# First chunks of an mLSTM and MLP-mixer kernel: zero fills ahead of the exponentials, gate subtractions on GpSimd, k q products ahead of phi, q factors sooner

## The chip, the cores and the metric

The kernel runs on one core of a Trainium2 chip. The metric is the device time of one execution in microseconds; before the change the median of three runs is 426.94 us (426.52 to 427.03). Five engines work in their own order and wait for one another by semaphores: TensorE (PE; its weight loads are listed as PEld), VectorE (DVE), ScalarE (ACT), GpSimd (POOL) and SyncE (SP), which issues nearly all DMAs.

## The reference

An mLSTM with exponential gates, whose output is the input x of a token mixer and a channel mixer.

```python
B, H, S, D = 4, 8, 768, 40
for t in range(S):
    m_new = np.maximum(f_gate[:, :, t] + m, i_gate[:, :, t])
    f_stab = np.exp(f_gate[:, :, t] + m - m_new)
    i_stab = np.exp(i_gate[:, :, t] - m_new)
    C = f_stab * C + i_stab * outer(v_t, k_t)
    n = f_stab * n + i_stab * k_t
    y[:, :, t] = sigmoid(o_t) * (C @ q_t) / max(abs(n @ q_t), 1)
x = y                                  # 4 x 768 x 320
h = np.maximum(x.T @ w_tok1, 0) @ w_tok2       # 768 -> 256 -> 768
u = x + h.T
out = u + np.maximum(u @ w_ch1, 0) @ w_ch2     # 320 -> 1536 -> 320
```

## The kernel before

The sequence is cut into six chunks of 128 steps for each of four batches; a unit (b, c) is a chunk c of batch b, and u0, u1, u2 are the first three chunks of batch 0. The gates of all batches and heads lie on 36 partitions with 768 steps along the free dimension. `gates_of` works out from them, on VectorE: a scan for the running maximum m (L120), f + m(t-1) - m(t) (L125, L127), a scan that sums these within a chunk to phi (L129), and b = i - m - phi (L131, L133). It is called once for chunks 0 and 1 and once for chunks 2 to 5. phi and b are the two planes of a tile z. `split` (L172) cuts z's fp32 values into three bf16 parts on three groups of partitions, so that products with 0/1 matrices can spread them exactly.

Within a chunk the output is (masked decay times k q products) times v, plus the carried state times q:

- `spread_late` and `spread_phi` (L163, L177) put phi(t) + b(s) of four heads into a PSUM bank "ps_phi" by products, with the mask of later steps; `spread_split` does both for eight heads. `prep_exp` (L287) takes the exponential on ScalarE into a tile dd.
- `st_s` (L307) makes the k q products "ps_sc" from a tile raw, in which two groups of four heads lie on partitions 0 to 39 and 64 to 103. With 64 rows in a product the rows up to 63 and 127 are read too, so `zero_rows` (L210) fills them with zeros, twice on ScalarE (raw1, raw2) and once on GpSimd (raw0).
- `st_p` (L317) multiplies dd by ps_sc on VectorE, in two halves; `st_pv` (L424) multiplies by v into "po".
- `spread_q` (L194) spreads phi for the factors of q into "ps_q" and, by `cols_w0`, the factors of k; `prep_q3` takes their exponentials on ScalarE (L274, and L142 for k) and scales q on GpSimd (L280); `prep_kw` scales k on GpSimd (L303).
- `st_state` (L368) multiplies the carried state by q (L378), and k by v for the new state (L386), which VectorE then masks and adds (L391, L395).
- `x0_ops` divides and multiplies by the sigmoid of the output gate (L476 to L485). `sigmoid` runs on ScalarE with another table of functions than the exponential, so a table load stands on either side.

PSUM is allotted in pools of two banks each: ps_h (phi, and the later ps_q), ps_s (k q products and chunk 1's ps_q), ps_m (po, pu, fillers), ps_acc. A tile waits for the readers of the tile that had its bank before.

All of it is written out in one fixed order of instructions for each engine: the order of the Python calls. The lines at the end of the function (from L862) are the first chunks' order; a loop then goes through chunks 1 to 5, while weights are loaded and decoded (`dec_...`), and the mixers of one batch run beside the attention of the next. `warm(n)` (L851) issues n products of zeros, whose result nobody reads, to keep TensorE at work.

DMAs on the sync queue are issued in program order too; each waits until the DMA eight places before it has landed, and until its target is free.

Of the kernel before, what the change touches and what calls it, by code (L numbers as in the profile page):

```python
# [18 lines left out]
L = 128  # L19
# [6 lines left out]
HP = 9  # L26
# [9 lines left out]
def kernel(ctx: ExitStack, tc: tile.TileContext, gates, qk, q3, kv, og,  # L36
# [16 lines left out]
    def load_sig(b, i):  # L53
        t = ap.tile([128, NC // 2, DM], F32, tag="sig", name="sig", bufs=3)
        nc.sync.dma_start(out=t, in_=og[b].rearrange("(c p) e -> p c e", p=128)[:, 3 * i:3 * i + 3, :])
        sig[(b, i)] = t
# [56 lines left out]
    bcol = wp.tile([128, NC, B * HP], F32, name="bcol")  # L113
    wcol = wp.tile([128, NC, B * HP], F32, name="wcol")

    def gates_of(c0, c1):
        lo, hi = c0 * L, c1 * L
        sl, sd, sm = slice(lo, hi), slice(max(lo, 1), hi), slice(max(lo, 1) - 1, hi - 1)
        v = nc.vector
        v.tensor_tensor_scan(m_t[:, sl], f_t[:, sl], i_t[:, sl],  # L120
                             -1e30 if lo == 0 else m_t[:, lo - 1:lo], op0=ALU.add, op1=ALU.max)
        yield
        if lo == 0:
            v.memset(f_t[:, 0:1], 0.0)
        v.tensor_tensor(f_t[:, sd], f_t[:, sd], m_t[:, sm], ALU.add)  # L125
        yield
        v.tensor_tensor(f_t[:, sd], f_t[:, sd], m_t[:, sd], ALU.subtract)  # L127
        yield
        v.tensor_tensor_scan(phi[:, sl], rst2[:, 0:hi - lo], f_t[:, sl], 0.0, op0=ALU.mult, op1=ALU.add)  # L129
        yield  # L130
        v.tensor_tensor(b_t[:, sl], i_t[:, sl], m_t[:, sl], ALU.subtract)  # L131
        yield
        v.tensor_tensor(b_t[:, sl], b_t[:, sl], phi[:, sl], ALU.subtract)  # L133
        yield

    def cols_w0(t, c):
        a, e = c * L, (c + 1) * L
        nc.tensor.matmul(t, top(z[:, 1, a:e]), id3, start=True, stop=False)
        nc.tensor.matmul(t, top(z[:, 0, e - 1:e]).to_broadcast([128, 128]), id3, start=False, stop=True)

    def cols_w0_out(t, c):
        nc.scalar.activation(wcol[:, c, 0:HP].rearrange("p (g i) -> p i g", g=3),  # L142
                             t.rearrange("p (i g) -> p i g", i=3), AF.Exp)
# [28 lines left out]
    def split(c0, c1, eng=nc.vector):  # L172
        p, r, r2 = (z[x:x + HP, :, c0 * L:c1 * L] for x in (0, 64, 96))
        eng.tensor_tensor(r, p, top(p), ALU.subtract)
        eng.tensor_tensor(r2, r, top(r), ALU.subtract)

    def spread_phi(r, c, h0=0, h1=H):  # L177
        zc = top(z[:, :, c * L:(c + 1) * L])
        for h in range(h0, h1):
            nc.tensor.matmul(r[h // 4][:, h % 4, :], id3[:, h:h + 1].to_broadcast([128, 128]),  # L180
                             zc[:, 0], start=False, stop=False)
            if h % 4 == 3:
                nc.tensor.matmul(r[h // 4], zc[:, 1], id3[:, h - 3:h + 1].unsqueeze(2).to_broadcast([128, 4, L]),
                                 start=False, stop=True)
# [25 lines left out]
    def zero_rows(i):  # L210
        for p in (32, 96):
            t = raws[i][p:p + 32].rearrange("p a h t -> p a (h t)")
            if i:
                nc.scalar.activation(t, zero[p:p + 32].unsqueeze(1).to_broadcast([32, 2, 512]), AF.Copy)
            else:
                nc.gpsimd.memset(t, 0.0)

    def sigmoid(b, r=range(2), part=slice(0, 3)):
        for i in r:
            t = sig[(b, i)][:, part]  # L220
            nc.scalar.activation(t, t, AF.Sigmoid)
# [65 lines left out]
    def prep_exp(u, hf):  # L287
        b, c = u
        dd = T[u]["dd"]
        if b == 0:  # L290
            nc.scalar.activation(dd[:, 4 * hf:4 * hf + 4, :], T[u]["phi"][hf], AF.Exp)  # L291
            return
        for h in range(4 * hf, 4 * hf + 4):
            nc.scalar.activation(dd[:, h, :], dd[:, h, :], AF.Exp, bias=bcol[:, c, HP * b + h:HP * b + h + 1])  # L294
# [9 lines left out]
                                wcol[:, c, HP * b:HP * b + H].unsqueeze(2).to_broadcast([128, H, D]), ALU.mult)  # L304
        t["kw"] = kw

    def st_s(u, mult=True, mid=iter(()), rows=64, pool=(ps_s, "s")):  # L307
        t = T[u]
        t["s"] = [pool[0].tile([128, 4, L], F32, tag=pool[1], name="ps_sc") for _ in range(2)]
        for h in range(4):  # L310
            for hf in range(2):
                r = t["raw"][64 * hf:64 * hf + rows]
                nc.tensor.matmul(t["s"][hf][:, h, :], r[:, 1, h, :], r[:, 0, h, :], start=True, stop=True)  # L313
        if mult:
            st_p(u, mid)
# [531 lines left out]
    def step(g, n=1):  # L847
        for _ in range(n):
            next(g, None)

    def warm(n, pool=(ps_m, "m"), z=zero):  # L851
        t = pool[0].tile([128, 512], F32, tag=pool[1], name="warm")
        for i in range(n):
            nc.tensor.matmul(t[:, 0:z.shape[-1]], z[:, 0:128], z, start=i == 0, stop=i == n - 1)  # L854
# [14 lines left out]
    load_sig(0, 0)  # L869
    load_qk(u1, 0)  # L870
    load_qk(u1, 1)
    load_sig(0, 1)
    load_kv(u1)
    q3s = {u1: load_q3t(u1)}

    T[u0]["phi"] = r = [spread_late(ps_h, "h") for _ in range(2)]
    warm(4)
    step(gates_of(0, 2), 9)
    split(0, 1)
    spread_phi(r, 0)  # L880
    t = ps_m.tile([128, HP], F32, tag="m", name="gw")
    cols_w0(t, 0)
    st_s(u0, mult=False, rows=D)
    split(1, 2)
    prep_exp(u0, 0)
    prep_exp(u0, 1)
    cols_w0_out(t, 0)
    zero_rows(2)
    prep_kw(u0)
    zero_rows(0)  # L890
    load_qk(u2, 0)
    load_qk(u2, 1)
    q3s[u2] = load_q3t(u2)
    load_kv(u2)
    dec_load(2)
    load_phi(us[3])
    load_qk(us[3], 0)
    load_qk(us[3], 1)
    spread_split(u1)
    st_s(u1, mult=False, pool=(ps_acc, "acc"))  # L900
    gr = gates_of(2, NC)
    step(gr, 3)
    st_p(u0)
    prep_exp(u1, 0)
    prep_exp(u1, 1)
    sigmoid(0)
    step(gr, 9)
    split(2, 3)
    warm(1)
    st_pv(u0)  # L910
    x0 = x0_ops(u0)
    step(x0, 2)
    st_state(u0)
    step(x0, 1)
    spread_q(u1, (ps_s, "s"))
    load_pq(u1, q3s[u1])
# [258 lines left out]
```

## Time and profile before

| what | value |
|---|---|
| median of 3 runs | 426.94 us |
| profiled execution | 426.81 us |
| its span, first to last instruction | 424.9 us |
| around the span | 1.9 us |
| granted TensorE clock, mean over the span | 1.000 |
| PE busy | 419.7 us (99%) |
| VectorE, ScalarE, GpSimd busy | 280.5, 184.0, 142.7 us |
| HBM read, written | 47.73 MB, 4.04 MB |

The table is from the page and the run list. The busy time of PE holds the fillers, and a product's end is modelled, so the starts of consecutive products tell more than their lengths. In a timeline a row merges instructions of one line that follow without a hole; a bracket gives the idle time ahead of it and what ended it. A wait that falls inside the modelled end of the previous product has no bracket; it shows as a late start.

### The profile page before, as it was taken

To read this page: it belongs to the slowest core of one execution; us is meant where nothing else is said; L and a number is where in the kernel's file an instruction comes from. 1 tells how busy PE (TensorE), PEld (TensorE's weight loads), DVE (VectorE), ACT (ScalarE), POOL (GpSimd) and SP (SyncE) were. 2 spreads that over 40 slices of the span, in tenths; PEclk is the share of its full clock that TensorE was granted. 3 is DMA by queue.
4 is the path that set the end of the run, shared out by engine and by line. 5 is a ranking of instruction groups with operands and counts; after the bars stand their busy time and mean duration, and the time that the engine had idled before them with its cause. 6 is when DMAs were issued, how large, how long until landed. Compare 5 with 4: busy or idle time off the path is not lost.

```text
span 424.9 us, 8988 instructions
## 1 busy us (share of the span) xinstructions
PE 419.7 (99%) x3510; PEld 396.8 (93%) x3510; DVE 280.5 (66%) x620; ACT 184.0 (43%) x426; POOL 142.7 (34%) x186
## 2 busy tenths in 40 slices
PE   8999999999999999999999999999999999999996
PEld 4888989999999999999999999999999999988996
DVE  8988565515876788799696698789796647111412
ACT  5978569893455635234323346334144112111211
POOL 7488488751544501241341230331350110000000
PEclk9999999999999999999999999999999999999999
DMA  7997658941876713333346121533320000000000
GB/s 218 278 292 268 241 170 290 272 147 52 253 199 195 213 39 104 123 117 125 95 154 195 35 93 43 137 116 93 119 86 32 0 23 12 0 2 0 35 28 31
DMA packets 24574, 52.34 MB, mean 123 GB/s; under 512 B 2565, under 2 KB 13325, under 8 KB 24533
## 3 DMA queue, kind: packets, MB, share of 16 engines
q1 hardware_dynamic: 24293, 51.61, 39.4%
q8 instruction: 27, 0.44, 0.5%
q10 hardware_dynamic: 240, 0.18, 0.1%
q14 instruction: 14, 0.11, 0.1%
HBM read 47.73 MB, written 4.04 MB: 122 GB/s over the span
## 4 chain that ended last, share of the span: by engine, by line
PE 94%; ACT 2%; POOL 2%; issue 0%; DVE 0%; POOLq 0%
PE acc L694 30%; PE ps_h L788 22%; PE ps_h L807 11%; PE ps_b L694 5%; PE ps_sc L313 5%; PE ps_a L694 5%; PE po L439 4%; PE po L409 3%; PE pu L386 3%; PE po L415 2%; PE po L378 1%; PE warm L854 1%; ACT dd L291 1%; PE ps_t L762 1%; PE ps_t L760 1%; PE ps_t L761 1%
## 5 line engine op out<-in xcount | busy, mean ns | idle before, releaser
L788 PE MATMUL ps_h<-uT,c1h 128*128 128x256 f32 x480 | 93.4, 282 | 0.0
L694 PE MATMUL acc<-c2h,gh 128*128 128x320 f32 x288 | 89.2, 319 | 0.0
L793 ACT ACTIVATE gh<-ps_h 128x512 fp32r<-128x512 f32 x48 | 28.7, 597 | 135.4 <-PE ps_h L788 132.4
L694 PE MATMUL acc<-c2l,gh 128*128 128x320 f32 x288 | 86.4, 309 | 0.0
L788 PEld LDWEIGHTS ps_h<-uT,c1h 128*128 128x128 f32 x480 | 76.9, 188 | 0.5
L788 PE MATMUL ps_h<-uT,c1l 128*128 128x256 f32 x288 | 74.3, 280 | 0.0
L794 DVE SCALAR_TENSOR_TENSOR gl<-ps_h,gh 128x512 fp32r<-128x512 f32 x48 | 33.0, 688 | 45.4 <-ACT gh L793 45.3
L694 PE MATMUL acc<-c2h,gl 128*128 128x320 f32 x288 | 61.8, 308 | 0.0
L694 PEld LDWEIGHTS acc<-c2h,gh 128*128 128x128 f32 x288 | 54.1, 188 | 1.6
L694 PEld LDWEIGHTS acc<-c2l,gh 128*128 128x128 f32 x288 | 54.2, 188 | 0.9
L788 PEld LDWEIGHTS ps_h<-uT,c1l 128*128 128x128 f32 x288 | 54.3, 188 | 0.0
L811 DVE SCALAR_TENSOR_TENSOR gl<-ps_h,gh 128x512 fp32r<-128x512 f32 x24 | 16.6, 692 | 49.0 <-ACT gh L810 49.0
L458 POOL TENSOR_TENSOR sig<-sig,ht 128x320 f32<-128x320 f32 x18 | 14.7, 816 | 98.4 <-DVE ht L419 90.0
L294 ACT ACTIVATE dd<-dd,bcol 128x128 f32<-128x128 f32 x144 | 45.8, 392 | 4.5 <-POOL dd L284 4.3
L694 PEld LDWEIGHTS acc<-c2h,gl 128*128 128x128 f32 x288 | 47.2, 188 | 0.0
L807 PE MATMUL ps_h<-uT,c1h 128*128 128x512 f32 x120 | 36.0, 394 | 0.0
L323 DVE TENSOR_TENSOR dd<-ps_sc,dd 128x512 f32<-128x512 f32 x48 | 30.9, 681 | 3.3 <-PE ps_sc L313 3.3
L509 POOL TENSOR_TENSOR xl<-x,xh 128x320 fp32r<-128x320 f32 x18 | 15.8, 877 | 51.1 <-DVE xh L507 46.3
L810 ACT ACTIVATE gh<-ps_h 128x512 fp32r<-128x512 f32 x24 | 14.3, 594 | 41.2 <-PE ps_h L807 41.2
L313 PE MATMUL ps_sc<-raw 64*128 64x128 f32 (+1 forms) x384 | 26.8, 282 | 0.0
L313 PEld LDWEIGHTS ps_sc<-raw 64*128 64x128 f32 (+1 forms) x384 | 23.1, 187 | 3.3 <-issue 1.7
L807 PEld LDWEIGHTS ps_h<-uT,c1h 128*128 128x128 f32 x120 | 22.1, 188 | 3.9
(152 smaller groups left out, 858.3 us busy)
## 6 DMA issues: line engine op xcount, KB each, us to landing
dd<-phi_d SPq DMA_DIRECT2D x18, 512.0 KB
wst<-in_wc_dram SPq DMA_DIRECT2D x22, 384.0 KB
kvt<-in_kv_dram SPq DMA_DIRECT2D x24, 324.0 KB
raw<-in_qk_dram SPq DMA_DIRECT2D x48, 160.0 KB
sig<-in_og_dram SPq DMA_DIRECT2D x8, 480.0 KB
out_dram<-x SPq DMA_DIRECT2D x24, 160.0 KB
q3t<-in_q_dram SPq DMA_DIRECT2D x20, 180.0 KB
wst<-in_wt_dram SPq DMA_DIRECT2D x8, 384.0 KB
```

Source lines behind the costliest of these rows:

```text
L294: nc.scalar.activation(dd[:, h, :], dd[:, h, :], AF.Exp, bias=bcol[:, c, HP * b + h:HP * b + h + 1])
L313: nc.tensor.matmul(t["s"][hf][:, h, :], r[:, 1, h, :], r[:, 0, h, :], start=True, stop=True)
L323: nc.vector.tensor_tensor(dd, t["s"][hf], dd, ALU.mult)
L439: nc.tensor.matmul(o, t["dd"][:, ROW[h], :], x, start=c == 0 and h == 0, stop=h == H - 1)
L458: nc.gpsimd.tensor_tensor(sg, sg, ht[:, :, 0:D], ALU.mult)
L509: nc.gpsimd.tensor_tensor(xl, x, f32(xh), ALU.subtract)
L694: nc.tensor.matmul(ps, a, m, start=(first and i == 0), stop=(last and i == n - 1))
L788: nc.tensor.matmul(ps[:, j, :], c1[x][:, a:a + 128], u[:, y, :], start=part is first and i == 0 and (order == 0 or j == 0), stop=i == len( ...
L793: nc.scalar.activation(gh, ps, AF.Relu)
L794: nc.vector.scalar_tensor_tensor(gl, ps, 0.0, f32(gh), op0=ALU.max, op1=ALU.subtract)
L807: nc.tensor.matmul(ps, c1[x][:, a:a + 128], u[:, :, y, :], start=n == 0, stop=n == len(todo) - 1)
L811: nc.vector.scalar_tensor_tensor(gl, ps, 0.0, f32(gh), op0=ALU.max, op1=ALU.subtract)
```

## The change

Nothing of what is computed changes. In the first chunks' order:

- both ScalarE zero fills stand at the start, ahead of chunk 0's exponentials; GpSimd's fill of raw0 is gone, and the products take 64 rows only in chunks 1, 2, 4 and 5 of batch 0, else the 40 filled by loads.
- the loads of q (for u1) go ahead of the second sigmoid load; the loads for u2 and the next chunk are issued earlier in the program.
- chunk 0's k q products stand ahead of the gates and of its phi products; one filler stands ahead of them where there were four.
- the gates of chunks 0 and 1 are split by one pair of operations on 256 steps instead of two pairs on 128.
- for the later chunks the scan of m still covers chunks 2 to 5; the f subtractions, phi scan and b subtractions are cut into chunk 2 (VectorE) and chunks 3 to 5, where GpSimd does the subtractions and VectorE the scan.
- chunk 1's `spread_q`, `prep_q3` and `prep_kw` stand ahead of chunk 0's `st_pv` and `st_state`, and the sigmoids behind chunk 1's q exponential; `x0_ops` of chunk 0 begins behind `st_state`.
- 13 fillers are left of 18.

On VectorE, from the scan of m for chunks 2 to 5 on, the kernel before has (z is the tile of phi and b, dd the decay, ps_sc the k q products):

```order
L120 SCALAR_TENSOR_TENSOR m_t<-f_t,m_t,i_t 36x512
L125 TENSOR_TENSOR f_t<-f_t,m_t 36x512
L127 TENSOR_TENSOR f_t<-f_t,m_t 36x512
L323 TENSOR_TENSOR dd<-ps_sc,dd 128x512 x2
L129 SCALAR_TENSOR_TENSOR z<-rst,f_t 36x512
L131 TENSOR_TENSOR z<-i_t,m_t 36x512
L133 TENSOR_TENSOR z<-z 36x512
L174 TENSOR_TENSOR z<-z 9x2x128
L175 TENSOR_TENSOR z<-z 9x2x128
```

and the changed kernel:

```order
L121 SCALAR_TENSOR_TENSOR m_t<-f_t,m_t,i_t 36x512
L128 TENSOR_TENSOR f_t<-f_t,m_t 36x128
L129 TENSOR_TENSOR f_t<-f_t,m_t 36x128
L132 SCALAR_TENSOR_TENSOR z<-rst,f_t 36x128
L137 TENSOR_TENSOR z<-i_t,m_t 36x128
L138 TENSOR_TENSOR z<-z 36x128
L324 TENSOR_TENSOR dd<-ps_sc,dd 128x512 x2
L132 SCALAR_TENSOR_TENSOR z<-rst,f_t 36x384
L178 TENSOR_TENSOR z<-z 9x2x128
L179 TENSOR_TENSOR z<-z 9x2x128
```

Chunk 0's multiplication (L323, now L324) had two operations between it and the scan and now has five shorter ones. On GpSimd, behind the constants, the kernel before has:

```order
L303 TENSOR_TENSOR kw<-kvt,wcol 128x320
L216 MEMSET raw_138 32x1024 x2
L279 COPY decay<-pq 120x3
L280 TENSOR_TENSOR q3t<-q3t,pq 120x384
L303 TENSOR_TENSOR kw<-kvt,wcol 128x320
L174 TENSOR_TENSOR z<-z 9x2x384
L175 TENSOR_TENSOR z<-z 9x2x384
```

and the changed kernel:

```order
L128 TENSOR_TENSOR f_t<-f_t,m_t 36x384
L129 TENSOR_TENSOR f_t<-f_t,m_t 36x384
L304 TENSOR_TENSOR kw<-kvt,wcol 128x320
L137 TENSOR_TENSOR z<-i_t,m_t 36x384
L138 TENSOR_TENSOR z<-z 36x384
L280 COPY decay<-pq 120x3
L281 TENSOR_TENSOR q3t<-q3t,pq 120x384
L304 TENSOR_TENSOR kw<-kvt,wcol 128x320
L178 TENSOR_TENSOR z<-z 9x2x384
L179 TENSOR_TENSOR z<-z 9x2x384
```

Two subtractions now stand ahead of chunk 0's scaled k (kw) and two behind it. On ScalarE, behind its first fill, the kernel before has:

```order
L291 ACTIVATE dd<-ps_phi 128x512 x2
L142 ACTIVATE wcol<-gw 128x3x3
L214 ACTIVATE raw_140<-zero 32x1024 x2
L291 ACTIVATE dd<-ps_phi 128x512 x2
L221 ACT_TABLE_LOAD
L221 ACTIVATE sig<-sig 128x960 x2
L274 ACT_TABLE_LOAD
L274 ACTIVATE pq<-ps_q 120x384
L142 ACTIVATE wcol<-ps_q 128x3x3
L291 ACTIVATE dd<-ps_phi 128x512 x2
```

and the changed kernel:

```order
L217 ACTIVATE raw_140<-zero 32x1024 x2
L292 ACTIVATE dd<-ps_phi 128x512 x2
L146 ACTIVATE wcol<-gw 128x3x3
L292 ACTIVATE dd<-ps_phi 128x512 x2
L275 ACTIVATE pq<-ps_q 120x384
L146 ACTIVATE wcol<-ps_q 128x3x3
L222 ACT_TABLE_LOAD
L222 ACTIVATE sig<-sig 128x960 x2
L292 ACT_TABLE_LOAD
L292 ACTIVATE dd<-ps_phi 128x512 x2
```

The q exponential of chunk 1 (pq) stood behind the sigmoids and stands ahead of them now, between the exponentials of chunks 1 and 2.

```diff
--- before.py
+++ after.py
@@ -113,25 +113,29 @@
     bcol = wp.tile([128, NC, B * HP], F32, name="bcol")
     wcol = wp.tile([128, NC, B * HP], F32, name="wcol")
 
-    def gates_of(c0, c1):
-        lo, hi = c0 * L, c1 * L
-        sl, sd, sm = slice(lo, hi), slice(max(lo, 1), hi), slice(max(lo, 1) - 1, hi - 1)
-        v = nc.vector
-        v.tensor_tensor_scan(m_t[:, sl], f_t[:, sl], i_t[:, sl],
-                             -1e30 if lo == 0 else m_t[:, lo - 1:lo], op0=ALU.add, op1=ALU.max)
-        yield
-        if lo == 0:
-            v.memset(f_t[:, 0:1], 0.0)
-        v.tensor_tensor(f_t[:, sd], f_t[:, sd], m_t[:, sm], ALU.add)
-        yield
-        v.tensor_tensor(f_t[:, sd], f_t[:, sd], m_t[:, sd], ALU.subtract)
-        yield
-        v.tensor_tensor_scan(phi[:, sl], rst2[:, 0:hi - lo], f_t[:, sl], 0.0, op0=ALU.mult, op1=ALU.add)
-        yield
-        v.tensor_tensor(b_t[:, sl], i_t[:, sl], m_t[:, sl], ALU.subtract)
-        yield
-        v.tensor_tensor(b_t[:, sl], b_t[:, sl], phi[:, sl], ALU.subtract)
-        yield
+    def cut(c0, c1):
+        return slice(c0 * L, c1 * L)
+
+    def gate_m(c0, c1):
+        lo = c0 * L
+        nc.vector.tensor_tensor_scan(m_t[:, cut(c0, c1)], f_t[:, cut(c0, c1)], i_t[:, cut(c0, c1)],
+                                     m_t[:, lo - 1:lo] if c0 else -1e30, op0=ALU.add, op1=ALU.max)
+
+    def gate_f(c0, c1, eng=nc.vector):
+        lo, hi = max(c0 * L, 1), c1 * L
+        if c0 == 0:
+            eng.memset(f_t[:, 0:1], 0.0)
+        eng.tensor_tensor(f_t[:, lo:hi], f_t[:, lo:hi], m_t[:, lo - 1:hi - 1], ALU.add)
+        eng.tensor_tensor(f_t[:, lo:hi], f_t[:, lo:hi], m_t[:, lo:hi], ALU.subtract)
+
+    def gate_phi(c0, c1):
+        nc.vector.tensor_tensor_scan(phi[:, cut(c0, c1)], rst2[:, 0:(c1 - c0) * L], f_t[:, cut(c0, c1)], 0.0,
+                                     op0=ALU.mult, op1=ALU.add)
+
+    def gate_b(c0, c1, eng=nc.vector):
+        sl = cut(c0, c1)
+        eng.tensor_tensor(b_t[:, sl], i_t[:, sl], m_t[:, sl], ALU.subtract)
+        eng.tensor_tensor(b_t[:, sl], b_t[:, sl], phi[:, sl], ALU.subtract)
 
     def cols_w0(t, c):
         a, e = c * L, (c + 1) * L
@@ -210,10 +214,7 @@
     def zero_rows(i):
         for p in (32, 96):
             t = raws[i][p:p + 32].rearrange("p a h t -> p a (h t)")
-            if i:
-                nc.scalar.activation(t, zero[p:p + 32].unsqueeze(1).to_broadcast([32, 2, 512]), AF.Copy)
-            else:
-                nc.gpsimd.memset(t, 0.0)
+            nc.scalar.activation(t, zero[p:p + 32].unsqueeze(1).to_broadcast([32, 2, 512]), AF.Copy)
 
     def sigmoid(b, r=range(2), part=slice(0, 3)):
         for i in r:
@@ -304,12 +305,12 @@
                                 wcol[:, c, HP * b:HP * b + H].unsqueeze(2).to_broadcast([128, H, D]), ALU.mult)
         t["kw"] = kw
 
-    def st_s(u, mult=True, mid=iter(()), rows=64, pool=(ps_s, "s")):
+    def st_s(u, mult=True, mid=iter(()), pool=(ps_s, "s")):
         t = T[u]
         t["s"] = [pool[0].tile([128, 4, L], F32, tag=pool[1], name="ps_sc") for _ in range(2)]
         for h in range(4):
             for hf in range(2):
-                r = t["raw"][64 * hf:64 * hf + rows]
+                r = t["raw"][64 * hf:64 * hf + (64 if u[0] == 0 and u[1] % 3 else D)]
                 nc.tensor.matmul(t["s"][hf][:, h, :], r[:, 1, h, :], r[:, 0, h, :], start=True, stop=True)
         if mult:
             st_p(u, mid)
@@ -861,6 +862,7 @@
 
     warm(10)
     zero_rows(1)
+    zero_rows(2)
     load_qk(u0, 0)
     load_qk(u0, 1)
     load_kv(u0)
@@ -869,56 +871,58 @@
     load_sig(0, 0)
     load_qk(u1, 0)
     load_qk(u1, 1)
+    q3s = {u1: load_q3t(u1)}
     load_sig(0, 1)
     load_kv(u1)
-    q3s = {u1: load_q3t(u1)}
-
-    T[u0]["phi"] = r = [spread_late(ps_h, "h") for _ in range(2)]
-    warm(4)
-    step(gates_of(0, 2), 9)
-    split(0, 1)
-    spread_phi(r, 0)
-    t = ps_m.tile([128, HP], F32, tag="m", name="gw")
-    cols_w0(t, 0)
-    st_s(u0, mult=False, rows=D)
-    split(1, 2)
-    prep_exp(u0, 0)
-    prep_exp(u0, 1)
-    cols_w0_out(t, 0)
-    zero_rows(2)
-    prep_kw(u0)
-    zero_rows(0)
     load_qk(u2, 0)
     load_qk(u2, 1)
     q3s[u2] = load_q3t(u2)
     load_kv(u2)
     dec_load(2)
     load_phi(us[3])
+
+    T[u0]["phi"] = r = [spread_late(ps_h, "h") for _ in range(2)]
+    warm(1)
+    st_s(u0, mult=False)
     load_qk(us[3], 0)
     load_qk(us[3], 1)
+    gate_m(0, 2)
+    gate_f(0, 2)
+    gate_phi(0, 2)
+    gate_b(0, 2)
+    split(0, 2)
+    spread_phi(r, 0)
+    t = ps_m.tile([128, HP], F32, tag="m", name="gw")
+    cols_w0(t, 0)
+    prep_exp(u0, 0)
+    prep_exp(u0, 1)
+    cols_w0_out(t, 0)
+    gate_m(2, NC)
+    gate_f(3, NC, nc.gpsimd)
+    gate_f(2, 3)
+    gate_phi(2, 3)
+    gate_b(2, 3)
+    prep_kw(u0)
     spread_split(u1)
     st_s(u1, mult=False, pool=(ps_acc, "acc"))
-    gr = gates_of(2, NC)
-    step(gr, 3)
     st_p(u0)
     prep_exp(u1, 0)
     prep_exp(u1, 1)
-    sigmoid(0)
-    step(gr, 9)
-    split(2, 3)
-    warm(1)
-    st_pv(u0)
-    x0 = x0_ops(u0)
-    step(x0, 2)
-    st_state(u0)
-    step(x0, 1)
     spread_q(u1, (ps_s, "s"))
     load_pq(u1, q3s[u1])
+    gate_phi(3, NC)
+    split(2, 3)
+    gate_b(3, NC, nc.gpsimd)
     prep_q3(u1)
     prep_kw(u1)
     split(3, NC, nc.gpsimd)
+    sigmoid(0)
     st_p(u1)
-    warm(3, (ps_h, "h"))
+    warm(2)
+    st_pv(u0)
+    st_state(u0)
+    x0 = x0_ops(u0)
+    step(x0, 2)
     spread_split(u2)
     prep_exp(u2, 0)
     prep_exp(u2, 1)
```

## Rows read from the trace of the kernel before

**Rows 1.** Page, part 1: busy time of each engine, share of span, instructions.

```profile
PE 419.7 (99%) x3510; PEld 396.8 (93%) x3510; DVE 280.5 (66%) x620; ACT 184.0 (43%) x426; POOL 142.7 (34%) x186
```

**Rows 2.** Timeline of PE, 0 to 45 us: start, length, what, count, idle before.

```profile
1.39 4.45 PE L854 MATMUL warm<-zero 128*128 128x512 bf16 x10 [1.39 <-POOL zero L61]
...
6.49 1.07 PE L854 MATMUL warm<-zero 128*128 128x512 bf16 x4
...
8.41 1.16 PE L313 MATMUL ps_sc<-raw 40*128 40x128 f32 x16
...
10.92 1.26 PE L313 MATMUL ps_sc<-raw 64*128 64x128 f32 x16
...
12.39 2.08 PE L439 MATMUL po<-kvt,dd 128*128 128x41 f32 x16
...
14.95 0.33 PE L198 MATMUL ps_q<-z,sel 128*120 128x128 bf16 x3
...
15.17 0.81 PE L854 MATMUL warm<-zero 128*128 128x512 bf16 x3
15.82 0.38 PE L165 MATMUL ps_phi<-late_b,id_b 128*128 128x512 bf16 x1
16.27 0.39 PE L180 MATMUL ps_phi<-z,id 128*128 128x128 bf16 x4
...
18.69 0.38 PE L198 MATMUL ps_q<-z,sel 128*120 128x128 bf16 x3
...
22.12 0.38 PE L165 MATMUL ps_phi<-late_b,id_b 128*128 128x512 bf16 x1
22.57 0.39 PE L180 MATMUL ps_phi<-z,id 128*128 128x128 bf16 x4
```

**Rows 3.** Timeline of ACT, 0 to 55 us.

```profile
3.50 2.13 ACT L214 ACTIVATE raw<-zero 32x1024 f32<-32x1024 bf16 x2
8.04 1.08 ACT L291 ACTIVATE dd<-ps_phi 128x512 f32<-128x512 f32 x2 [2.40 <-PE ps_phi L183]
...
12.48 1.28 ACT L221 ACT_TABLE_LOAD   x1
13.78 1.90 ACT L221 ACTIVATE sig<-sig 128x960 f32<-128x960 f32 x2
...
16.99 0.49 ACT L274 ACTIVATE pq<-ps_q 120x384 f32<-120x384 f32 x1
...
19.14 0.49 ACT L274 ACTIVATE pq<-ps_q 120x384 f32<-120x384 f32 x1 [0.26 <-PE ps_q L139]
```

**Rows 4.** Timeline of DVE, 0 to 55 us.

```profile
6.76 0.42 DVE L175 TENSOR_TENSOR z<-z 9x256 f32<-9x256 f32 x1
7.21 0.69 DVE L174 TENSOR_TENSOR z<-z 9x256 f32<-9x256 f32 x1
...
8.63 1.28 DVE L120 TENSOR_TENSOR_SCAN m_t<-f_t,m_t,i_t 36x512 f32<-36x512 f32 x1
9.94 1.03 DVE L125 TENSOR_TENSOR f_t<-f_t,m_t 36x512 f32<-36x512 f32 x1
...
11.61 1.27 DVE L323 TENSOR_TENSOR dd<-ps_sc,dd 128x512 f32<-128x512 f32 x2
...
13.94 0.66 DVE L131 TENSOR_TENSOR z<-i_t,m_t 36x512 f32<-36x512 f32 x1
```

**Rows 5.** Timeline of POOL, 0 to 55 us.

```profile
2.16 0.29 POOL L85 TENSOR_SCALAR_AFFINE_SELECT late<-late 128x128 f32<-128x128 f32 x1
...
3.03 0.70 POOL L85 TENSOR_SCALAR_AFFINE_SELECT eye<-eye 128x128 f32<-128x128 f32 x1
...
9.28 1.14 POOL L303 TENSOR_TENSOR kw<-kvt,wcol 128x320 f32<-128x320 f32 x1 [0.91 <-ACT wcol L142]
...
17.75 1.01 POOL L280 TENSOR_TENSOR q3t<-q3t,pq 120x384 f32<-120x384 f32 x1
18.72 0.72 POOL L303 TENSOR_TENSOR kw<-kvt,wcol 128x320 f32<-128x320 f32 x1
```

## The prediction

> **What bounds the kernel now.** I read the page's busy shares first: TensorE is busy 99% of the span [rows 1]. A microsecond is therefore won or lost only where TensorE waits or runs filler. I then read TensorE's timeline, and after it those of the engines that release it. The edit ends within the first 25 us; from the second batch on the order is unchanged, so a lead or a delay at 22 us is taken to reach the end one to one. The reader is to see in [rows 2] how few holes there are: 18 filler products (10, 4, 1 and 3; the three larger groups are shown), and two waits in front of phi products. The one of chunk 2 starts 0.45 us behind L165, the one of chunk 3 also 0.45 us (22.12 to 22.57). A 512-column product passes in 0.22 us (three fillers fill 15.17 to 15.82), so each wait is 0.23 us.
>
> **The change part by part.** All sums are on the profiled execution: 426.81 us, a span of 424.9 us with 1.9 us around it, 0.13 us under the median of 426.94.
>
> Fills. Two ScalarE fills of 2.13 us move from behind chunk 0's exponentials to ahead of them. They fit the 2.40 us in which ScalarE idles before 8.04 [rows 3], so there they cost nothing; had the idle time gone, they would cost up to 2.13. Chunk 1's exponentials come 1 to 2 us sooner by it. The GpSimd fill goes too; nothing on TensorE waited for it. The padded 64 rows become 40 in more chunks: 1.16 us at 40 rows, 1.26 at 64 with a start behind a load [rows 2]. I take 0; the ends are -0.1 and +0.1 us.
>
> Loads. The q load of chunk 1 goes one place forward in SP's queue, the third chunk's loads are issued sooner, and the second sigmoid load and chunk 1's k v load go one place back. The loads of chunk 1's k and q keep their place. Their products began at 10.92 without idle time [rows 2], so they had landed by then and no more is known. ScalarE comes to the sigmoids later than now, which covers the load put back; uncovered it would cost its own place in the queue, under 1 us. I take 0.
>
> TensorE's order. Chunk 0's k q products (1.1 us) replace three fillers (0.65 us) ahead of phi, then chunk 1's phi and k q products follow, which end near 12.05: the loads' time 10.92 plus 1.1. What is new stands behind them: L198's three broadcast products for chunk 1's q factors, at 14.95 now [rows 2], move ahead of the state products. They write into the bank from which VectorE reads chunk 0's k q products, so they wait for the first half of that multiplication (L323, at 11.61 now [rows 4]). Everything of TensorE is queued behind them. Call their start S.
>
> From S two chains run to the next L198 (chunk 2, at 18.69 now), which needs a bank that the first of chunk 2's exponentials frees.
> ScalarE: 0.45 until the q exponential starts (18.69 to 19.14), 0.6 for it with the small one behind it (estimate from 0.49), 1.28 table load, 1.90 sigmoids, 1.28 for the second load, as long as the one shown [rows 3], 0.55 for half of the two exponentials' 1.08, and 0.08 for the hand-overs: 6.14 us.
> TensorE: of the 6.30 us between 12.39 and 18.69 [rows 2] take off L198's group 0.22, the fillers 0.65, the wait 0.23 and a wait of 0.1 between the halves at 12.39; add L198's group and two fillers, 0.22 and 0.43. That is 5.75 us.
> So ScalarE ends last, the next L198 starts at S + 6.14, and the wait of 0.23 at 22.57 goes, because GpSimd's split, which ended it, runs sooner. (If it stays, 0.23 is lost.) The change breaks even at S = 18.69 + 0.23 - 6.14 = 12.8.
>
> When S comes is VectorE's matter. Chunk 2's scan starts at 8.63 now; the split of chunks 0 and 1 in one pair instead of two saves two fixed parts. With 0.42 for 256 elements and 0.66 for 512 [rows 4] a fixed part is about 0.18 us, so the scan starts near 8.25 and ends near 9.53. Then come four operations of 128 elements, 0.30 each, a scan of 128 at 0.32 to 0.40, and gaps: 1.7 us, to 11.2. The multiplication's first half and its hand-over take 0.7, so S would be 11.9, and 12.05 behind the k q products.
>
> But GpSimd now works beside it. Its two subtractions of 384 elements wait for the same scan, then kw, then the next subtraction. Where both engines read, the trace shows them taking turns. GpSimd's select of 128x128 takes 0.29 alone and 0.70 beside a VectorE scan; kw takes 0.72 alone and 1.14 beside the scan that ends at 9.91; and the VectorE sum behind that scan takes 1.03, where its like takes 0.66 [rows 4, 5]. So kw costs VectorE 0.37. For 384 full elements no such pair is shown; kw alone is 0.72 and the product of 384 is 1.01 [rows 5], so I scale 0.37 to 0.52. The smallest collision shown is 0.27 (0.69 against 0.42 [rows 4]); the largest takes GpSimd's whole remaining time, 0.51 of kw (9.91 to 10.42), scaled 0.72. VectorE's operations behind the scan meet GpSimd four times: second f operation, scan of 128 and second b operation at 0.52 each, and the first b operation against kw at 0.37, which I weigh half since it does not wait for the scan ahead of it. That is 1.74. S = 11.9 + 1.74 = 13.64, which is 0.84 past break-even: 426.81 + 0.84 = 427.65, rounded to 427.7. What is late next is TensorE itself: 5.75 against 6.14 leaves it 0.4 of idle time behind chunk 2's products as well.
>
> The Trainium skill (SBUF — State Buffer, "SBUF: two separate sides") speaks against this edit: a VectorE operation with two inputs in SBUF and a GpSimd operation that reads SBUF hold a shared port pair by turns, and the one that starts second "fully blocks" for the whole instruction. The trace agrees on the turns, but VectorE was free after 0.37 of kw's last 0.51 us. By the rows the sum is 1.74, by the rule 2.7, which is a rival below.
>
> **The rivals.**
> No collision that counts. If GpSimd's operations on 36 partitions hold nothing up, S is 12.05 and the time 426.81 - 0.75 = 426.1. For it: much of GpSimd's work beside VectorE in the trace is slowed by nothing. Against it: the pairs of [rows 4, 5], which are the same kinds of operation. It decides from S below 12.8. Should the k q loads land before 10.92, it could gain 0.2 more.
> Small collisions. Three at the smallest shown, 0.27: S = 12.7, and 426.7, no change. For it: 128 elements are short. Against: GpSimd has an operation waiting at each turn.
> Whole turns. VectorE waits for all that remains of each GpSimd operation: three at 0.72 and kw at 0.51, S = 11.9 + 2.67 = 14.57, and the time 426.81 + 1.77 = 428.6. It decides if VectorE's second f operation takes over 1 us. By the rule of the skill page named above this is the case to expect.
> TensorE's clock falls. At the start ten fillers take 4.45 us, the lower of the two levels, 1.2 GHz; from 6.49 four take 1.07, the upper, 2.4 GHz [rows 2]. Five fillers go, and TensorE idles up to 1.6 us ahead of S. Should it then run at the lower level for as long as at the start (1.39 to 6.49), it loses up to half of 5.1 us: 427.7 + 2.5 = 430.2. Against it: no such fall behind the short waits shown. The Trainium skill (TensorE: Matmul & The Clock Gate, "What's actually happening") has the lower level as the default that activity lifts; no run here shows what would undo it.
>
> **How the numbers follow.** Forecast (427.2 to 428.1) 0.42; no collision 0.20; small collisions 0.20; whole turns 0.10; clock 0.05; others 0.03. About 0.2% (0.85 us) is what a measurement of this kernel can tell from no change, so 426.09 and 427.79 are the limits. Slower: 0.4 of the forecast's chance, all of whole turns and clock, some of the rest, 0.33. Faster: most of the no-collision case and a little of the others, 0.18. Same: 0.49. The range from 426.0 to 428.6 leaves out about 1 in 10 on either side; the forecast's own is 427.2 to 428.1.
>
> **What would show it.** VectorE's second 128-element f operation and its scan of 128 should take 0.8 and 0.9 us instead of 0.30 and 0.4; the multiplication of chunk 0 should start near 12.9 instead of 11.61; L198 of chunk 1 should start near 13.6, after an idle stretch of TensorE of about 1.5 us released by VectorE; chunk 2's exponentials should start near 19.2 behind the second table load; L198 of chunk 2 near 19.8; and no wait on GpSimd ahead of chunk 3's phi. Short 128-element operations and an L198 near 12.1 would make the prediction wrong on the faster side; a TensorE stretch at half rate behind 12 us, on the slower.

## The result, and the profile after

The changed kernel takes 430.87 us, the median of 4 runs (430.6 to 432.47), against 426.92 (426.52 to 427.03, 4 runs): a ratio of 1.0102, with an interval of 1.0077 to 1.0127. It is 3.95 us slower, 3.2 us over the forecast and 2.3 us beyond the range. The profiled execution took 430.83 us, its span is 429.1 us (before 424.9), and its mean granted clock is 0.991 (the four runs: 0.988 to 0.992; before 1.000).

Busy time of each engine, from the page; it answers to [rows 1]:

```profile
PE 421.3 (98%) x3505; PEld 399.0 (93%) x3505; DVE 280.6 (65%) x619; ACT 183.7 (43%) x426; POOL 144.2 (34%) x188
```

TensorE has five products fewer than before and is busy 1.6 us longer. Its timeline answers to [rows 2]; L198 is now L202 (a chunk's broadcast products), L165 and L180 are L169 and L184 (phi), L439 is L440 (output products):

```profile
8.22 0.39 PE L184 MATMUL ps_phi<-z,id 128*128 128x128 bf16 x4 [0.33 <-DVE z L179]
...
10.92 1.52 PE L314 MATMUL ps_sc<-raw 64*128 64x128 f32 x16
14.51 0.33 PE L202 MATMUL ps_q<-z,sel 128*120 128x128 bf16 x3 [2.06 <-DVE dd L324]
...
15.16 3.23 PE L440 MATMUL po<-kvt,dd 128*128 128x41 f32 x16
...
23.25 0.38 PE L202 MATMUL ps_q<-z,sel 128*120 128x128 bf16 x3
...
26.68 0.38 PE L169 MATMUL ps_phi<-late_b,id_b 128*128 128x512 bf16 x1
26.89 0.39 PE L184 MATMUL ps_phi<-z,id 128*128 128x128 bf16 x4
```

Three things are to be seen. L202 of chunk 1 starts at 14.51, behind 2.06 us of idle time that VectorE's multiplication ended. The same 16 output products that took 2.08 us before take 3.23. And chunk 3's phi products start at 26.89 where they stood at 22.57: 4.32 us later, about the lengthening of the span (4.2 us). So the whole loss is made by then. The same stretch in windows (start:end, length, busy time and instructions of PE, PEld, DVE, ACT, POOL, then the granted clock, the DMA share and GB/s):

```profile
12.00:14.00 2.00, 0.44 (x7) 0.38 (x5) 1.97 (x4) 0.00 (x0) 1.71 (x2) 1.00 1.06 327
14.00:16.00 2.00, 1.49 (x13) 1.34 (x13) 1.97 (x4) 1.07 (x3) 0.00 (x0) 0.85 0.98 251
16.00:18.00 2.00, 2.00 (x12) 2.00 (x11) 1.94 (x3) 1.99 (x3) 1.94 (x3) 0.50 0.70 263
18.00:22.00 4.00, 4.00 (x20) 2.76 (x20) 2.98 (x9) 2.57 (x3) 3.84 (x4) 0.50 0.99 269
22.00:24.00 2.00, 2.00 (x26) 1.77 (x26) 0.58 (x1) 1.26 (x3) 0.96 (x2) 0.94 0.77 274
```

From 12 to 14 us TensorE is busy for 0.44 of 2.00 us; behind it the granted clock is 0.50, the lower level of 1.2 GHz, from 15.42 to 22.25 us. In the kernel before, it is 1.00 throughout these windows. VectorE's timeline, which answers to [rows 4]:

```profile
8.21 1.47 DVE L121 TENSOR_TENSOR_SCAN m_t<-f_t,m_t,i_t 36x512 f32<-36x512 f32 x1
9.71 0.29 DVE L128 TENSOR_TENSOR f_t<-f_t,m_t 36x128 f32<-36x128 f32 x1
10.03 0.97 DVE L129 TENSOR_TENSOR f_t<-f_t,m_t 36x128 f32<-36x128 f32 x1
11.03 1.16 DVE L132 TENSOR_TENSOR_SCAN z<-rst,f_t 36x128 f32<-36x128 f32 x1
12.12 0.74 DVE L137 TENSOR_TENSOR z<-i_t,m_t 36x128 f32<-36x128 f32 x1
12.89 0.96 DVE L138 TENSOR_TENSOR z<-z 36x128 f32<-36x128 f32 x1
13.78 1.27 DVE L324 TENSOR_TENSOR dd<-ps_sc,dd 128x512 f32<-128x512 f32 x2
```

and GpSimd's, for [rows 5]:

```profile
9.76 1.09 POOL L128 TENSOR_TENSOR f_t<-f_t,m_t 36x384 f32<-36x384 f32 x1 [1.10 <-DVE m_t L121]
10.93 0.99 POOL L129 TENSOR_TENSOR f_t<-f_t,m_t 36x384 f32<-36x384 f32 x1
11.88 0.83 POOL L304 TENSOR_TENSOR kw<-kvt,wcol 128x320 f32<-128x320 f32 x1
12.68 1.03 POOL L137 TENSOR_TENSOR z<-i_t,m_t 36x384 f32<-36x384 f32 x1
```

The second f operation on VectorE could start at 10.03; GpSimd's L128 runs until 10.85, and VectorE's operation ends at 11.00. Each of the next three ends behind a GpSimd operation in the same way: the scan behind L129 (11.92), L137 behind kw (12.71), L138 behind GpSimd's L137 (13.71). Chunk 0's multiplication starts at 13.78, 2.17 us later than before. ScalarE, for [rows 3]:

```profile
3.49 4.29 ACT L217 ACTIVATE raw<-zero 32x1024 f32<-32x1024 bf16 x4
...
14.91 0.49 ACT L275 ACTIVATE pq<-ps_q 120x384 f32<-120x384 f32 x1 [3.29 <-PE ps_q L143]
...
20.93 0.60 ACT L292 ACTIVATE dd<-ps_phi 128x512 f32<-128x512 f32 x1 [0.95 <-PE ps_phi L187]
```

The fills lie in idle time, as priced. But chunk 2's exponential, which the forecast had behind the second table load, waits for TensorE, which runs at half rate.

### The profile page after: what moved, and what is told of

It is laid out like the page before. It is cut to its first block, busy times and chain, and to the rows that moved or that the text cites. A ratio compares the mean times of both kernels' runs of the same rounds, so it can differ in the third digit from the quotient of the medians.

```text
span 429.1 us, 8973 instructions
## 1 busy us (share of the span) xinstructions
PE 421.3 (98%) x3505; PEld 399.0 (93%) x3505; DVE 280.6 (65%) x619; ACT 183.7 (43%) x426; POOL 144.2 (34%) x188
## 4 chain that ended last, share of the span: by engine, by line
PE 92%; DVE 2%; POOL 2%; DMA 2%; ACT 1%; issue 1%; SPq 0%; POOLq 0%
PE acc L695 29%; PE ps_h L789 20%; PE ps_h L808 10%; PE ps_b L695 5%; PE po L440 5%; PE ps_a L695 5%; PE ps_sc L314 5%; PE pu L387 3%; PE po L410 3%; PE po L416 2%; DMA dd<-phi_d 2%; PE po L379 2%; PE ps_t L763 1%; PE ps_t L762 1%; PE ps_t L761 1%
## 5 line engine op out<-in xcount | busy, mean ns | idle before, releaser
L324 DVE TENSOR_TENSOR dd<-ps_sc,dd 128x512 f32<-128x512 f32 x48 | 31.0, 682 | 4.7 <-PE ps_sc L314 4.5
L314 PEld LDWEIGHTS ps_sc<-raw 40*128 40x128 f32 (+1 forms) x384 | 23.5, 188 | 4.3 <-issue 2.4
L314 PE MATMUL ps_sc<-raw 40*128 40x128 f32 (+1 forms) x384 | 27.4, 283 | 0.1
```

The costliest lines, as they stand in the source:

```text
L324: nc.vector.tensor_tensor(dd, t["s"][hf], dd, ALU.mult)
```

## The experiments

Each kernel was timed beside the kernel before on the same chip: 427.34 us in the first group (the first four), 427.15 in the second (the next four), 427.16 in the third. "Broadcast" gives the starts of the broadcast products of chunks 1 and 2 in the profiled execution; the last column counts the executions whose mean granted clock was under 0.998. Kernels of different groups are compared by what each loses to its own kernel before.

| kernel | us | ratio to before (interval) | broadcast | clock |
|---|---|---|---|---|
| changed kernel | 430.87 | 1.0102 (1.0077 to 1.0127) | 14.51, 23.25 | 4 of 4 |
| 1 gates on VectorE | 428.39 | 1.0029 (1.0018 to 1.0040) | 12.97, 21.42 | 3 of 10 |
| 2 wait filled | 428.47 | 1.0032 (1.0016 to 1.0047) | 14.64, 20.78 | 0 of 9 |
| 3 reads that nobody needs | 430.59 | 1.0086 (1.0065 to 1.0108) | 14.32, 21.66 | 5 of 6 |
| 4 writes that nobody needs | 428.27 | 1.0028 (1.0016 to 1.0040) | 12.48, 19.34 | 1 of 9 |
| 5 chunk 2 first | 427.38 | 0.9998 (0.9987 to 1.0008) | 12.08, 18.27 | 0 of 12 |
| 6 fills alone | 427.44 | 0.9997 (0.9985 to 1.0010) | 15.17, 18.78 | 0 of 12 |
| 7 split sooner | 431.09 | 1.0066 (1.0038 to 1.0093) | 12.27, 18.46 | 4 of 7 |
| 8 VectorE late | 431.11 | 1.0092 (1.0070 to 1.0115) | 14.28, 20.42 | 6 of 6 |
| 9 sigmoids early | 431.29 | 1.0073 (1.0048 to 1.0099) | 12.41, 17.96 | 5 of 7 |
| 10 no fillers | 431.20 | 1.0095 (1.0079 to 1.0112) | 12.28, 17.65 | 5 of 5 |

**1, gates on VectorE.** The later chunks' subtractions go from GpSimd to VectorE, behind chunk 0's multiplication.

```
-    gate_f(3, NC, nc.gpsimd)
     gate_f(2, 3)
...
     split(2, 3)
-    gate_b(3, NC, nc.gpsimd)
+    gate_b(3, NC)
```

(`gate_f(3, NC)` now stands ahead of `gate_phi(3, NC)`.)

> The changed kernel with the four subtractions of chunks 3 to 5 back on VectorE, behind chunk 0's multiplication. Theory 1 (turns at the memory): without GpSimd's reading operations VectorE's 128-element operations take 0.3 us again but for one that meets kw, the multiplication of chunk 0 starts near 11.3 instead of 13.78, L202 of chunk 1 near 12.1 to 12.4 instead of 14.51, TensorE idles under 0.5 us there and keeps the upper clock level, and the time is 426.1 to 426.5 us. Theory 2 (the order itself): L202 ahead of chunk 0's state products makes TensorE wait whatever GpSimd does; L202 stays near 14 and the time near 430.9.

VectorE's timeline, then TensorE's:

```profile
10.54 0.28 DVE L129 TENSOR_TENSOR f_t<-f_t,m_t 36x128 f32<-36x128 f32 x1
10.85 0.96 DVE L132 TENSOR_TENSOR_SCAN z<-rst,f_t 36x128 f32<-36x128 f32 x1
11.74 0.26 DVE L137 TENSOR_TENSOR z<-i_t,m_t 36x128 f32<-36x128 f32 x1
12.03 0.28 DVE L138 TENSOR_TENSOR z<-z 36x128 f32<-36x128 f32 x1
```

```profile
12.97 0.33 PE L202 MATMUL ps_q<-z,sel 128*120 128x128 bf16 x3 [0.18 <-DVE dd L324]
...
17.54 0.57 PE L184 MATMUL ps_phi<-z,id 128*128 128x128 bf16 x4 [1.19 <-DVE z L179]
```

The operations of 128 steps are short again (only the scan beside kw is not), and the wait in front of L202 is 0.18 instead of 2.06. L202 comes at 12.97 and not at 12.1 to 12.4, because all of this execution stands 0.7 us later from chunk 0's first phi product on (8.93 against 8.22). The time that was expected, 426.1 to 426.5, did not come. What this kernel still loses has another place: it put chunk 2's split behind two f operations (0.54 and 0.55 us) and a scan that takes 1.64 us beside GpSimd's q3t and kw (0.94 in the changed kernel), and chunk 2's phi waits 1.19 us for it. In this profiled execution the clock was at 0.50 behind that wait, from 17.59 to 21.00, so the 21.42 of the table holds a loss that 7 of its 10 executions don't have; kernel 4, with the same order and the clock held, has 19.34.

**2, wait filled.** The changed kernel with nine filler products ahead of L202; the collisions stay.

```
+    warm(9)
     spread_q(u1, (ps_s, "s"))
```

> The changed kernel with nine fillers (0.22 us each, 1.9 us) in the wait ahead of L202 of chunk 1. Theory 1 (the idle stretch lets the clock fall, on top of the late multiplication): L202 stays at 14.5, no stretch at the lower level behind 15 us, the next L202 near 20.7 instead of 23.25, and the time is 428.3 us (430.87 less 2.6). Rival (the clock falls for another cause, such as the many small products): it falls all the same and the time stays at 430.9.

```profile
12.53 2.12 PE L855 MATMUL warm<-zero 128*128 128x512 bf16 x9
14.64 0.33 PE L202 MATMUL ps_q<-z,sel 128*120 128x128 bf16 x3
...
20.78 0.33 PE L202 MATMUL ps_q<-z,sel 128*120 128x128 bf16 x3 [0.56 <-ACT dd L292]
```

```profile
16.00:18.00 2.00, 2.00 (x21) 1.88 (x21) 1.90 (x4) 1.99 (x3) 1.80 (x3) 1.00 0.64 240
```

L202 comes as late as in the changed kernel, the granted clock stays at 1.00, and chunk 2's broadcast products follow 6.14 us later instead of 8.74. So 2.60 us of the loss is the clock. Timed against its own kernel before, this one loses 1.13 us where the changed kernel loses 3.95: nine products that compute nothing take about 2.8 us off. (The profiled execution took 430.11 us, more than the median; chunk 3's phi starts at 24.38 in it, 1.81 behind before, and what else it lost stands far behind these chunks.)

**3 and 4, reads and writes that nobody needs.** Kernel 1, with GpSimd given three subtractions of 36x384 at the old places, into a weight tile that is loaded later (3), or four zero fills of 36x1024 instead (4).

```
+    extra(2)    # 3: nc.gpsimd.tensor_tensor(c2[1][...], i_t[...], m_t[...], ALU.subtract)
+                # 4: nc.gpsimd.memset(f32(c2[1][...]), 0.0)
     gate_f(2, 3)
...
     prep_kw(u0)
+    extra(1)    # 4: extra(2)
```

> As e1, but GpSimd does three subtractions of 36x384 into a tile of weights that is overwritten later, in the places where the changed kernel has its own; nothing waits for them but the later writer. Theory 1 (turns at the memory): VectorE's short operations take 0.7 to 1.2 us as in the changed kernel, L202 is near 14 to 14.5, the clock falls, and the time is 430.5 to 431. Rival (VectorE waited for GpSimd's results): no result is waited for here, so it runs as e1, 426.1 to 426.5.

> As e1, but GpSimd does four memsets of 36x1024 (0.95 us each by the fills of the kernel before) in the same places: as much GpSimd time as in the changed kernel, without a read. Theory 1 (turns between operations that read): as e1 within 0.3 us, VectorE's short operations 0.3 us but for the one beside kw. Rival (any GpSimd work holds VectorE up): VectorE's short operations take 0.7 us and more, and the time is 428 to 431.

Kernel 3, VectorE, then GpSimd, then TensorE (its L206 is L202 above):

```profile
9.83 0.97 DVE L129 TENSOR_TENSOR f_t<-f_t,m_t 36x128 f32<-36x128 f32 x1
...
12.70 0.96 DVE L142 TENSOR_TENSOR z<-z 36x128 f32<-36x128 f32 x1
```

```profile
9.56 2.17 POOL L137 TENSOR_TENSOR c2l<-i_t,m_t 36x384 fp32r<-36x384 f32 x2 [1.10 <-DVE m_t L121]
```

```profile
14.32 0.33 PE L206 MATMUL ps_q<-z,sel 128*120 128x128 bf16 x3 [2.40 <-DVE dd L328]
```

Kernel 4, VectorE, then GpSimd:

```profile
9.85 0.28 DVE L129 TENSOR_TENSOR f_t<-f_t,m_t 36x128 f32<-36x128 f32 x1
...
11.26 0.26 DVE L141 TENSOR_TENSOR z<-i_t,m_t 36x128 f32<-36x128 f32 x1
```

```profile
8.42 1.95 POOL L137 MEMSET c2l<- 36x1024 f32 x2
...
11.00 1.95 POOL L137 MEMSET c2l<- 36x1024 f32 x2
```

Operations whose results nobody waits for bring back the long VectorE operations to the hundredth (0.97 and 0.96, as in the changed kernel); fills on the same engine at the same time leave 0.28 and 0.26. So it is neither a dependency nor GpSimd's being busy. What the fills lack is the reading of SBUF. The Trainium skill (SBUF — State Buffer, "SBUF: two separate sides") says it so: a VectorE operation with two inputs in SBUF and a GpSimd operation that reads SBUF exclude each other for a whole instruction. These runs agree: 0.97 and 0.96 us beside the subtractions, 0.28 and 0.26 beside the fills. The time of kernel 4 fits both of its theories (428.27; 428 to 431 was the rival's); the lengths of the operations decide.

**5, chunk 2 first.** The changed kernel with the scan of m cut, chunk 2 alone ahead of chunk 0's multiplication; the other chunks' scan and f operations behind chunk 2's split on VectorE, GpSimd left with their b operations; chunk 0's output operations ahead of chunk 1's multiplication.

```
-    gate_m(2, NC)
-    gate_f(3, NC, nc.gpsimd)
+    gate_m(2, 3)
...
+    split(2, 3)
+    gate_m(3, NC)
+    gate_f(3, NC)
     gate_phi(3, NC)
...
```

> Chunk 2's gates alone ahead of chunk 0's multiplication, the scan of the later chunks and their f operations behind it on VectorE, GpSimd left with the last two b operations and the split. Theory (turns of the two engines make S late, and the idle stretch in front of S drops TensorE's clock): VectorE meets GpSimd nowhere but in kw, S near 12.1 with an idle stretch under 0.3 us, no half-rate stretch, next three broadcast products 6.1 us later at 18.2, against 18.69 in the kernel before, and the wait of 0.23 gone: 0.7 us less than before, ratio 0.998. Rival (the new order itself, q factors of chunk 1 ahead of the state products and the sigmoids behind them, costs time): S near 12.1 all the same, but chunk 2's products begin no sooner than 18.9, ratio 1.001 or more.

```profile
9.56 0.42 DVE L132 TENSOR_TENSOR_SCAN z<-rst,f_t 36x128 f32<-36x128 f32 x1
```

```profile
12.08 0.38 PE L202 MATMUL ps_q<-z,sel 128*120 128x128 bf16 x3
...
18.27 0.33 PE L202 MATMUL ps_q<-z,sel 128*120 128x128 bf16 x3 [0.57 <-ACT dd L292]
...
20.15 0.80 PE L387 MATMUL pu<-kvt,kw 128*120 128x123 f32 x6 [0.62 <-issue]
...
22.91 0.39 PE L184 MATMUL ps_phi<-z,id 128*128 128x128 bf16 x4
```

With only one turn left ahead of the multiplication (the second b operation beside kw, 0.80 us) L202 starts at 12.08, and the next 6.19 us later, 0.42 ahead of the kernel before. Then a wait of 0.62 us, for which the trace names nothing, but which ends right behind VectorE's output operations of chunk 0 (20.04), takes the lead back: chunk 3's phi starts at 22.91, 0.34 behind before. The new order with nearly no collisions is level with the old; the expected 0.7 us did not come.

**6, fills alone.** The kernel before with `zero_rows(2)` ahead of the exponentials.

> The kernel before with one edit of the change alone: the two zero fills of the third raw tile on ScalarE ahead of the exponentials. Theory (fills lie in ScalarE's idle time and only chunk 1's exponentials come sooner, which nothing on TensorE waits for): everything from 12.39 on in its old place within 0.1 us, ratio 0.9995 to 1.0002. Rival (the fills decide when chunk 1's multiplication, the split and so the phi of chunk 3 come): the wait of 0.23 us ahead of chunk 3's phi goes, ratio 0.9994 or less.

```profile
22.21 0.38 PE L165 MATMUL ps_phi<-late_b,id_b 128*128 128x512 bf16 x1
22.43 0.39 PE L180 MATMUL ps_phi<-z,id 128*128 128x128 bf16 x4
```

The two starts are 0.22 apart, so the wait of 0.23 is gone, as the rival had it; but the ratio is 0.9997, and its interval holds 1. Any gain is too small to tell.

**7, split sooner.** Kernel 1 with `split(2, 3)` ahead of the two f operations.

> The kernel of the first experiment (the later chunks' gates on VectorE, behind chunk 0's multiplication) with chunk 2's split moved ahead of the two f subtractions of the later chunks. Theory (the 1 us that experiment still lost against before is the 1.35 us in which chunk 2's phi products wait for that split): the wait goes, phi of chunk 2 begins near 16.2 instead of 17.5, the next broadcast products near 19.0 to 19.4, no half-rate stretch, ratio 0.999 to 1.001. Rival (the loss sits in ScalarE's later sigmoids or in VectorE's load later on): ratio stays at 1.002 to 1.004.

```profile
19.86 0.92 PE L379 MATMUL po<-Cn,q3t 120*128 120x164 f32 x6 [1.04 <-DVE Cn L392]
21.40 1.42 PE L387 MATMUL pu<-kvt,kw 128*120 128x123 f32 x6 [0.62 <-POOL z L179]
```

Chunk 2's phi no longer waits, and its broadcast products come at 18.46; this part held. But what had been pushed in front of phi is now in front of chunk 1's products, which wait 0.56, 1.04 and 0.62 us between 17.9 and 21.4 us. In the profiled execution the clock then fell from 21.19 to 28.02. Of 7 executions 3 kept the clock and took 428.0 to 428.6 us; 4 lost it and took 431.1 to 431.7. Where the clock held, the time is still 0.9 to 1.4 us over the kernel before (427.15): by its waits the loss sits in VectorE's load later on, which the rival named.

**8, VectorE late.** Kernel 7 with two VectorE fills ahead of chunk 0's multiplication, and nothing more on GpSimd.

```
+    for _ in range(2):
+        nc.vector.memset(f32(c2[1][0:B * HP, 0:1024]), 0.0)
     st_p(u0)
```

> The kernel with the split moved forward (the one sent with this) and two VectorE memsets of 36x1024, about 0.9 us each, ahead of chunk 0's multiplication: VectorE late by 1.8 us with no work of GpSimd in it. Theory (what costs the clock is the idle stretch alone, whoever causes it): S near 14.6 with an idle stretch of 1.9 to 2.2 us, TensorE at half rate for some us from 15 to 17 on, and 3 to 4.5 us more than the same kernel without the memsets. Rival (the clock falls for what GpSimd does, or for the kind of product behind S): S just as late, clock full, 1.7 us more at most.

```profile
14.28 0.33 PE L202 MATMUL ps_q<-z,sel 128*120 128x128 bf16 x3 [1.80 <-DVE dd L324]
```

```profile
16.00:18.00 2.00, 2.00 (x21) 1.76 (x21) 1.95 (x2) 1.99 (x3) 1.57 (x2) 1.00 0.71 240
...
24.00:26.00 2.00, 2.00 (x12) 2.00 (x11) 1.85 (x7) 2.00 (x6) 2.00 (x4) 0.50 1.06 323
```

This was expected wrongly in part. All 6 executions lost clock (means 0.988 to 0.996), without any added work on GpSimd, so GpSimd isn't needed for it. But in the profiled one the clock held behind the wait of 1.80 us and fell only at 23.82, behind the waits of kernel 7, which this kernel shares; so the run doesn't price the first wait by itself. Its median is that of kernel 7 (431.11 and 431.09), where 3 to 4.5 us more had been expected.

**9 and 10.** Kernel 5 with the sigmoids ahead of chunk 1's q exponential, and the later b operations and chunk 3's split on VectorE behind chunk 1's multiplication (9); the same without `warm(2)` (10).

> Chunk 2's gates first, as in the kernel that came out level with before, and two more moves: the sigmoids ahead of the q exponential again (ScalarE idled 0.9 us there), and the later chunks' b operations with chunk 3's own split on VectorE behind chunk 1's multiplication, so that chunk 0's output operations come sooner. Theory (that kernel lost its lead of 0.4 us at 18.27 to two waits behind it: 0.57 for ScalarE's second table load, 0.62 for VectorE's late output operations): chunk 2's exponentials start near 16.8, the next broadcast products near 17.7 without a wait, no wait ahead of the state products of chunk 1, chunk 3's phi products near 21.5 against 22.57 in the kernel before, no half-rate stretch: 1 us less than before, ratio 0.9975. Rival (VectorE's load up to chunk 3's phi is the bound, in whatever order): chunk 3's split or chunk 1's multiplication ends late and takes the lead back, chunk 3's phi at 22.5 to 23, ratio 0.9995 to 1.001.

> The kernel sent with this, without the two filler products behind chunk 1's broadcast products (0.43 us). Theory (TensorE is the bound up to the next broadcast products once ScalarE is early): 0.2 to 0.4 us less than with them, the state products of chunk 0 at 12.4 instead of 12.8. Rival (the fillers hold the clock): a half-rate stretch behind 13 us, 1.5 us or more lost. If ScalarE or VectorE ends last, no difference.

Kernel 9, TensorE, then VectorE:

```profile
17.96 0.38 PE L202 MATMUL ps_q<-z,sel 128*120 128x128 bf16 x3
...
27.21 1.34 PE L387 MATMUL pu<-kvt,kw 128*120 128x123 f32 x6 [1.53 <-POOL w1l L689]
```

```profile
26.62 0.49 DVE L486 TENSOR_TENSOR x<-po,den 128x320 f32<-128x320 f32 x1
```

Up to chunk 3's phi the theory held (exponentials of chunk 2 at 16.44, no wait ahead of L202, which is 0.73 ahead of before; chunk 3's phi at 21.80, 0.77 ahead). Then VectorE, loaded with what had been moved behind, ends chunk 1's output operation at 27.1, where it ended at 24.7 before, and L387, chunk 2's products for the state, starts right behind it, although the trace names an earlier GpSimd operation. In the profiled execution the clock fell at that wait (0.82 from 26 to 28 us, then 0.50), and 5 of 7 executions lost clock; the two others took 428.4 us, so the order alone costs over 1 us too. The rival had the cause, VectorE's load, but not the place: it takes the lead back behind chunk 3's phi and not ahead of it. Kernel 10 shows it again: its output products of chunk 0 come 0.56 sooner, phi of chunk 3 waits 0.57 for VectorE, and the time is the same. The granted clock is 1.00 up to 26 us, so the two fillers were not what held it at 13.

No version beats the kernel before.

## Why the prediction was wrong

The direction of the middle value was right (though no change had the best chance, 0.49), the mechanism of the forecast was there, and its size was too small; the loss that made three fifths of the whole had been given 1 chance in 20.

- **Fills, loads, k q products, wait on GpSimd's split.** As priced. The fills lie in ScalarE's idle time (3.49 to 7.78), chunk 1's k q products begin at 10.92 as before, the scan starts at 8.21 (8.25 forecast), and the wait ahead of chunk 3's phi is gone (26.68 to 26.89 is 0.21).
- **The collisions, 1.74 ("I scale 0.37 to 0.52").** This term failed by its size. Alone the four VectorE operations take 0.28, 0.42, 0.26 and 0.28 (kernels 1 and 5); here 0.97, 1.16, 0.74 and 0.96. That is 2.59 us of turns, against 2.67 for the whole-turn rival and 1.74 for the forecast; S was 14.51, where the rival had 14.57 and the forecast 13.64. The row that the forecast scaled, the sum behind kw, was taken for a partial turn, because VectorE lost 0.37 of kw's last 0.51 us. But that sum ran until 10.97, 0.55 us behind the end of kw, and its like takes 0.66 in all: it was a whole turn. From the start of the VectorE operation kw had 0.48 left, 0.11 more than was lost; the four operations here lose 0.69, 0.74, 0.48 and 0.68 of 0.82, 0.89, 0.59 and 0.82 left, 0.11 to 0.15 less each time. So the loss is what GpSimd has left less a nearly constant 0.11 to 0.15, and not a share of it. Kernel 3 gives S at 6.29 us behind chunk 0's first phi product L184 (here its L188), the changed kernel 14.51 - 8.22 = 6.29 as well. That S came so near the rival's is partly luck: the scan of m collided too, beside GpSimd's L107 (1.47 instead of 1.28 us), which the forecast had not counted, and the short operations with their gaps were about as much shorter than priced.
- **S + 6.14.** Right where the clock is held: 6.14 in kernel 2, 6.19 in kernel 5. The break-even at S = 12.8 gives 14.51 - 12.8 = 1.71 us of loss without the clock; in kernel 2 chunk 3's phi is 1.81 late, and its time is 0.7 to 2.0 us over its kernel before by the interval.
- **The clock, chance 0.05.** This step failed by its argument, which was "no such fall behind the short waits shown". The waits shown were 0.23 us; the one that the forecast itself put ahead of S was 1.5, and it became 2.06. Waits so much shorter say nothing about it. The price was near, 2.5 said and 8.74 - 6.14 = 2.60 measured, but that is luck: it was half of a stretch of 5.1 us, and the stretch lasted 6.83, half of which is 3.4. TensorE had 0.56 us to spare ahead of chunk 2's broadcast products (kernel 2); the rest of the difference is not accounted for. The rivals were also priced each for itself, while a longer collision makes the wait ahead of S longer; together they are 1.71 + 2.60 = 4.31, and 4.32 is what chunk 3's phi shows. A joint case of whole turns and clock would have been 431.1.

What stays open: whether the clock falls behind a given wait differs between executions of one kernel (kernels 1, 3, 4, 7 and 9), and kernel 8 kept it behind 1.80 us. Falls came only in kernels whose trace has a wait of TensorE of over 1 us in this part (1.04 in kernel 7 to 2.40 in kernel 3), and none came in kernels 2, 5 and 6, whose longest wait behind 8 us is 0.6 us. Filling the wait of the changed kernel kept the clock in 9 of 9 executions. The runs don't show what decides it from one execution to the next.

## What to carry to other kernels

Before work goes to GpSimd to relieve VectorE, pair every operation of both that reads SBUF in that stretch, and charge VectorE with nearly all that remains of GpSimd's. In these traces VectorE's multiplication, which has one input in PSUM (1.29 us for two beside GpSimd's q3t, 1.27 with GpSimd idle), and GpSimd's fills are free of it. A wait of TensorE longer than any that the profile shows isn't priced by its length alone: ask what half rate behind it would cost, and if the wait can't go, fill it. An order that gains at one wait on a loaded engine is followed to the next thing that this engine owes, since there the gain was taken back each time.

## What the runs showed of the hardware

- A VectorE scan takes turns too: 0.42 us alone (kernel 5) and 1.16 beside GpSimd's subtraction, for 36x128.
- GpSimd's fills don't: 0.28 beside them and alone (kernel 4).
- A VectorE operation that meets a reading GpSimd operation shows as a longer operation, not as idle time: in five pairs it takes what GpSimd has left, less 0.11 to 0.15 us, on top of its own time.
- The half-rate stretch of the changed kernel lasts 6.83 us and costs 2.60; that of kernel 3 lasts 3.41 (16.52 to 19.93), and its two broadcast starts are 7.34 apart, 1.20 more than with the clock held. Over executions of one kernel the time comes in two groups, 428.0 to 428.6 and 431.1 to 431.7 in kernel 7, with mean granted clocks of 0.999 to 1.000 and 0.992.
